# A fused attention, routing and channel-mix kernel: every tile's buffer from a table, routing's compare on GpSimd, and a new hand-written order

## The chip, the cores and the metric

The kernel runs on one core of a Trainium2 chip. The metric is the device time of one execution in microseconds, as the median of several runs. The engines are named TensorE (PE in the profile), VectorE (DVE), ScalarE (ACT), GpSimd (POOL) and SyncE (SP), the last of which only issues transfers here.

## The reference, cut to what matters

Three layers follow each other. The first is attention with hashed buckets, 2 batches, 8 heads, 768 rows, 64 columns a head. The second is a mixture of 4 attention experts with causal masks, of which each row uses the two with the largest gate logits. The third is a channel mix with a hidden width of 1,024.

```python
# layer 1: scores only where the sign bits of q and k under proj agree
q_bits = (einsum('bhsd,dk->bhsk', q, proj) > 0); k_bits = ...
scores = where(q_bucket == k_bucket, q @ k.T / 8, -1e9)
x = softmax(scores) @ v
# layer 2: top 2 of 4 experts by x @ w_gate
for e in range(4):
    a = softmax(causal((x @ wq[e]) @ (x @ wk[e]).T / 8))
    out += gate_weight(e) * (a @ (x @ wv[e]) @ wo[e])
# layer 3: x_prev is x moved down by one row
xk = mu_k * x + (1 - mu_k) * x_prev;  xr = mu_r * x + (1 - mu_r) * x_prev
return sigmoid(xr @ w_r) * (relu(xk @ w_k) ** 2 @ w_v)
```

The weights of layer 3 come as 64-bit floats.

## The kernel before, in words

The rows are worked on in 12 units of 128 (6 per batch). Nearly every matrix is held as the sum of two 16-bit parts, a high one and a low one, so that three 16-bit matmuls give one precise product. A high part is a cast (mostly ScalarE), a low part is a subtraction (VectorE or GpSimd).

The steps of a unit i are these. `prep` and `hash_` (lines 477 to 495) load the query tile, split it (tile `naq`), turn it on TensorE and make hash signs. `score(h)` (line 545) makes one head's scores in PSUM (tile `s`, two slots), and `softmax` (line 518) takes the masked minimum on VectorE (tile `P`), the exponential on ScalarE, the high part (`PHL`), the low part on GpSimd (`PHL<-P,PHL`), and has a transfer turn both (`PT<-PHL`). `pv(h)` (line 562) multiplies with the values (tile `x`). `moe_steps` (line 602) does the same for the experts. Its `proj_v` (line 634) also makes the gate logits in PSUM (tile `vg`) and the routing: VectorE copies the logits out (`lg`), GpSimd subtracts all pairs and adds a constant for ties (`gt`, lines 659 and 660), VectorE compares with zero (line 661) and counts (`rk`, lines 662 and 663), and forms the gate product (`g`, line 666). `mix_steps` (line 768) is layer 3: `shift`, eight `hidden` blocks (matmul tile `h`), four `gate` blocks (`r`) and eight `down` blocks (`v`, into the output tile `e`).

The keys and values of a batch are split once (`key_steps`, line 418): `half` makes the key tiles (`nak`, `nbk`, `y2`), `hash_` their hash signs (`z_k`, which need the split projection `prhl`, lines 285 to 290) and `y1`, and `vals` (line 456) splits the values (`v<-v,v` on VectorE, 128x768, with two inputs in SBUF). The layer-3 weights are put together from their 64-bit halves by `split_d` (line 355): one ScalarE, one GpSimd and four VectorE operations for each of 20 blocks of 128x512, besides a cast.

All operations are first recorded as objects, one list in program order. `arrange` (line 179) reads a table of 2,566 numbers and puts them into the order in which they are issued (`ORDER`, line 865): that order alone sets how the engines' queues interleave, and each engine then works through its own queue in order. Transfers in go through SyncE's queue, except the constants, the projection and the two mixing vectors, which go through ScalarE's queue.

Tiles come from pools. `b2` (2 KB a partition, 18 slots) holds most of a unit's work, `b3` (13 slots) the softmax tiles, `b4` (4 KB, 3 slots) raw weights and the hidden activations `k2`. PSUM has four banks under the tag `d` and two two-bank slots for scores. The layer-3 weights WK2, WV2 and WR have tiles of their own for the whole kernel (40 KB a partition). Before, a tile takes the slot of its tag that the framework gives it at issue.

Of the kernel before, what the change touches and what calls it, by code (L numbers as in the profile page):

```python
# [869 lines left out]
mM|OUKyfUA)o?H5!Jg0_IzSUBi9?_wR>#Kp8`i-C&<5(_J{Uox=q6@>KcNAPp;A~ABhhGzOf_&lG{J+=8#+QGXo|OREak_)VJ`dyw{aYer+Lr<>tQpDLIto5  # L870
7Q{jrmF{3$D2xyA5In^Ba2OupS6l!K;TyKaXw(kg;Su<b1>ISAjGbTuY=k~=7w_Rw_<`r3Ikv)<7?WD#1e!z>={^2Iu_!jhp~+Mq7g1qX)V0I*xR^G<W_XTA
X$$m)#n>6*(s4Ke9q<Eo#9j#W5x2r8JP+~c1r~9|+%|ZLeeoDXr~7yn;uDk51-J;ku@8Fcf}POO6zYndF$p2{$Io~Yp5QAy1;^+gSVG6?HNL^2pwth$VGj(n
l-5yVBKm?)(dc)4i_fqpPNnXclrBL+8iK{$-&Dd4z~PvH#$ZWzg08_bx(p-mIxMH5xSpobSR97qa5|l&2y_Qx&|bO$|G`Zdh~serCZj8`k2cV3ib!{%kSpa9
(N-FXqi`brfg9-*y?3K=65fOT^e>!-IaJyur@3?sw$W|aL@6jGy@4n2tNX=G##A&22jgEf1=G+poQgB(03D<<?hM?A)HILM(+4-7GSPILfirOyK7bYU5Vq4w
%1X6eI!a4FQ$~6OvvCg2#m6uVX3`;AKu;kvWufepgFd-`=ubLK3&~-BHy?j@=V%@-z*Y3oWuP7O*)7CH_!hpp=B}(eLeJniynrS65>`_=w-Ud(7H&0`cY7!&
t-`ZZl=9LV+DW@;7FBTBi18J)bh+q@D?m%}H<ypTJK*J5jF#bfdJXN}7J3Ko;fGsGn@P}P3HlR1zy(@^A3<?|+fA)pLCQ}RU2!T&t=(T(h$^|l^a%#Kb^JG%
qTCelGkk#*_%Bs)$fxNHT_nesC=a!9rRg#m4su_ij;lZ&Tt({Wn6FR+SJhRbYAym2H+1W{2wkOXbc3!_cPD&@%1~MQg}%XHw}Gp>lz5B2Lt8h*MZ`|-KU#~O
T@P2+)pMz^9F?cr)X4n+z%H(_yGfoa(_MN_!yMuZdPOg(iCck$_vk)Vq4!jks?krpk*iZpszJ3VHCA@@T|2jl(_mWM%v*S*+sggiPxzW@xL@fFHFXau64s{3
PPwN`hriKw{zTjO1HGm67#U+=GuPFv#~A!KZp293%YCNaF7QYCLN(nZ>f^prRvzkxyC@hHqhU;p%rQAS)}dIO0FB?#H>&08QzP2JyLbb}=1sVhck^LRh?_AA
$HH|Ofge*n%EommJ0IaD)R;!O9DI}?&@paGTW}k0#~pZ$<MaQc;=a=l+KJs<U-yKz;!}!^&nOY*<XlW{7skOj>|9*D&hfAT9p|{*R?h2$aD(F`J8=nkH}1tf  # L880
# [73 lines left out]
```

## Time and profile before

| what | us |
|---|---|
| median of 3 runs | 506.62 (505.15 to 506.81) |
| the profiled execution, its own time | 508.27 |
| its span, first to last instruction | 506.5 |
| busy in the span: TensorE, VectorE, ScalarE, GpSimd | 440.5, 371.2, 340.8, 317.8 |
| mean granted TensorE clock, as a share of full speed | 0.952 |

In the rows further down, an instruction is named by what it writes and reads (`P<-s`), by names in the program with buffer numbers left out. Line 188 is the one place that issues everything, so all rows have that line and are told apart by their tiles. A time in brackets after `idle before` is how long the engine had nothing to do ahead of it, and the name behind the arrow is what ended it.

### The profile page before, as it was taken

The page shows a single profiled execution, that of the slowest core. Times are in us where ns is not written, and L with a number is a line of the kernel's source. Part 1 is how long each engine was busy: PE and PEld are TensorE (multiplying, and loading weights), DVE is VectorE, ACT ScalarE, POOL GpSimd, SP SyncE. Part 2 cuts the span into 40 slices and gives each one's busy share as a digit, 9 for nine tenths or more (in the row PEclk, how much of TensorE's full clock was granted, in tenths as well). Part 3 has the DMA queues.
Part 4 walks back from the last instruction along what each step waited for, and adds up shares of the span by engine and source line. Part 5 has one row for each costly group of instructions (what it writes and reads, how often), then busy time and mean ns, then how long its engine had stood idle before and what let it go on. Part 6 is the DMA issues. An engine that isn't in the chain of part 4 may idle for free.

```text
span 506.5 us, 15492 instructions
## 1 busy us (share of the span) xinstructions
PE 440.5 (87%) x6288; PEld 334.7 (66%) x6288; DVE 371.2 (73%) x1010; ACT 340.8 (67%) x646; POOL 317.8 (63%) x309
## 2 busy tenths in 40 slices
PE   3663588786879999999989999899899999999996
PEld 2641367574666767767765887587687867886753
DVE  4899788999988867999788579576867554554412
ACT  4259478668887987667868886866786856662411
POOL 2659977775795785857758956745876752452200
PEclk9996578897989999999999999999999999999999
DMA  8699979899989998964989687977983890645011
GB/s 274 165 249 204 174 173 166 217 187 215 167 198 193 180 162 189 182 120 91 156 178 183 128 136 137 150 143 112 160 146 72 135 156 6 106 65 147 1 64 41
DMA packets 224856, 75.06 MB, mean 148 GB/s; under 512 B 216208, under 2 KB 220432, under 8 KB 224784
## 3 DMA queue, kind: packets, MB, share of 16 engines
q1 hardware_dynamic: 223280, 73.95, 76.4%
q8 instruction: 49, 0.80, 0.7%
q10 hardware_dynamic: 1504, 0.11, 0.2%
q14 instruction: 23, 0.19, 0.1%
HBM read 22.14 MB, written 3.15 MB: 50 GB/s over the span
## 4 chain that ended last, share of the span: by engine, by line
PE 46%; DMA 6%; DVE 6%; ACT 4%; issue 3%; POOL 2%; SPq 1%; DVEq 0%; POOLq 0%; ACTq 0%
PE h L188 10%; PE v L188 9%; PE r L188 5%; PE s L188 5%; PE x L188 4%; DMA PT<-PHL 4%; PE qk L188 2%; PE se L188 2%; PE y L188 2%; PE o L188 2%; ACT P L188 2%; PE vg L188 2%; POOL PHL L188 1%; PE tr_y L188 1%; DVE P L188 1%
## 5 line engine op out<-in xcount | busy, mean ns | idle before, releaser
L188 POOL TENSOR_TENSOR PHL<-P,PHL 128x768 f16<-128x768 f32 x96 | 159.0, 1664 | 33.8 <-ACT PHL L188 28.2
L188 DVE TENSOR_SCALAR_CACHE_REDUCE P<-s 128x768 f32<-128x768 f32 x96 | 90.9, 950 | 16.2 <-DMA PT<-PHL 4.8
L188 ACT ACTIVATE P<-P,mx 128x768 f32<-128x768 f32 x96 | 89.1, 929 | 15.8 <-DVE mx L188 15.4
L188 PE MATMUL s<-y,x 128*128 128x384 f16 x384 | 83.2, 348 | 10.9 <-DVE P L188 8.5
L188 PE MATMUL h<-mk,WK 128*128 128x128 f16 x1152 | 75.5, 221 | 3.4 <-DVE WV L188 2.4
L188 PE MATMUL x<-v,PT 128*128 128x64 f16 x1728 | 68.0, 199 | 11.5 <-DMA PT<-PHL 7.3
L188 PEld LDWEIGHTS <-PT 128*128 128x128 f16 x1728 | 63.1, 102 | 20.1 <-DMA PT<-PHL 9.3
L188 PEld LDWEIGHTS <-WK 128*128 128x128 f16 x1152 | 69.2, 99 | 8.5 <-issue 4.1
L188 PE MATMUL v<-WV,k 128*128 128x512 f16 x288 | 71.1, 379 | 0.4 <-DVE WV L188 0.4
L188 PEld LDWEIGHTS <-x 128*128 128x128 f16 x576 | 42.6, 102 | 41.1 <-issue 17.4
L188 ACT ACTIVATE PHL<-P 128x768 f16<-128x768 f32 x72 | 60.1, 837 | 11.9 <-DMA PT<-PHL 3.2
L188 POOL TENSOR_TENSOR PHL_m<-P_m,PHL_m 128x512 f16<-128x512 f32 (+2 forms) x24 | 33.8, 1413 | 27.4 <-ACT PHL_m L188 26.7
L188 PEld LDWEIGHTS <-k 128*128 128x128 f16 x288 | 26.4, 98 | 24.7 <-issue 0.6
L188 PE MATMUL r<-WR,mr 128*128 128x512 f16 x144 | 37.6, 385 | 0.0
L188 PE MATMUL qk<-xT,WQK 128*128 128x128 f16 x576 | 37.2, 219 | 0.3 <-DVE xT L188 0.3
L188 PEld LDWEIGHTS <-WQK 128*128 128x128 f16 x576 | 33.9, 98 | 3.5 <-issue 0.7
L188 POOL TENSOR_SCALAR PHL<-P 128x768 f16<-128x768 f32 x24 | 20.3, 846 | 15.0 <-ACT P L188 7.1
L188 DVE SCALAR_TENSOR_TENSOR h<-h,t 128x512 f32<-128x512 f32 x24 | 16.6, 693 | 13.2 <-ACT t L188 13.1
L188 DVE TENSOR_SCALAR_CACHE_REDUCE P_m<-se 128x512 f32<-128x512 f32 (+2 forms) x24 | 19.4, 818 | 8.8 <-PE se L188 5.0
L188 DVE COPY x<-tr_x 128x512 f16<-128x512 f16 x48 | 19.4, 417 | 6.9 <-PE tr_x L188 6.8
L188 ACT ACTIVATE t<-h 128x512 f32<-128x512 f32 x24 | 14.1, 588 | 14.2 <-PE h L188 13.8
L188 ACT ACTIVATE P_m<-P_m,bias_m 128x512 f32<-128x512 f32 (+2 forms) x24 | 19.7, 821 | 5.7 <-DVE P_m L188 5.5
(133 smaller groups left out, 854.6 us busy)
## 6 DMA issues: line engine op xcount, KB each, us to landing
raw_k<-in_moe_w_k_dram SPq DMA_DIRECT2D x8, 512.0 KB, 4.7
raw_v<-in_moe_w_v_dram SPq DMA_DIRECT2D x8, 512.0 KB, 4.3
q<-in_q_dram SPq DMA_DIRECT2D x12, 256.0 KB, 5.0
k<-in_k_dram SPq DMA_DIRECT2D x8, 384.0 KB, 4.9
v<-in_v_dram SPq DMA_DIRECT2D x8, 384.0 KB, 4.3
...
PT<-PHL SPq DMA_TRANSPOSE x96, 4.2
```

The costliest lines, as they stand in the source:

```text
L188: getattr(getattr(self.nc, engine), method)(*[real(a) for a in args], **{k: real(a) for k, a in kw.items()})
```

## The change

It has six parts.

- `arrange` takes a second table, HOMES, with one number for each tile that has a tag. The tile's tag becomes the tag and that number, with one buffer, so that each tile's slot is set beforehand and not by rotation.
- The weights WK2, WR and WV2 are no longer tiles of their own but 20 blocks of 2 KB in `b2`, which has 40 slots instead of 18. The matmuls read them block by block.
- The hidden activations `k2` are two tiles in `b2` (high and low) instead of one in `b4`, which has 2 slots instead of 3.
- Routing's comparison with zero runs on GpSimd, as a compare and a multiplication by one.
- The ranks are written to a part of the PSUM bank of the value projection (`pw[:, 416:420]`) instead of to SBUF. The gate product reads them there.
- ORDER is a new table for the same operations. It was made by a planner that counts the locks of the port that VectorE and GpSimd share.

```diff
-    def arrange(self, table):
-        places = np.frombuffer(zlib.decompress(base64.b85decode("".join(table.split()))), np.uint16)
-        self.order = [self.ops[i] for i in places]
+    def arrange(self, table, homes):
+        def unpack(text, dt):
+            return np.frombuffer(zlib.decompress(base64.b85decode("".join(text.split()))), dt)
+        self.order = [self.ops[i] for i in unpack(table, np.uint16)]
+        tiles = {}
+        for o in self.ops:
+            for t in o.uses:
+                tiles.setdefault(t, len(tiles))
+        for t, h in zip(tiles, unpack(homes, np.uint8)):
+            if t.slot:
+                t.kw.update(tag=f"{t.slot[1]}_{h}", bufs=1)
...
-    NB2, NB3, NB4, NX2 = 18, 13, 3, 4
+    NB2, NB3, NB4, NX2 = 40, 13, 2, 4
...
-    WK2 = cp.tile([P, NC, 2, DFF], F16, name="WK2")
-    WV2 = cp.tile([P, NF, 2, DM], F16, name="WV2")
-    WR = cp.tile([P, NC, 2, DM], F16, name="WR")
+    WK2, WV2, WR = {}, {}, {}
+
+    def block(d, key, nm):
+        def part(hl):
+            if key not in d:
+                d[key] = sp.tile([P, 2, WN], F16, tag="b2", bufs=NB2, name=nm)
+            return d[key][:, hl, :]
+        return part
...
-                    w_k[c * P:(c + 1) * P, m:m + WN], lambda hl: WK2[:, c, hl, m:m + WN], SWK, f"k2{c}_{m}"))
+                    w_k[c * P:(c + 1) * P, m:m + WN], block(WK2, (c, m), f"WK2_{c}_{m}"), SWK, f"k2{c}_{m}"))
...
-            nc.vector.tensor_scalar(gt, gt, 0.0, None, op0=OP.is_lt)
-            rank = sp.tile([P, E], F32, tag="rk", name=f"rk_{i}")
+            nc.gpsimd.tensor_scalar(gt, gt, 0.0, 1.0, op0=OP.is_lt, op1=OP.mult)
+            rank = pw[:, 416:416 + E]
             nc.vector.tensor_reduce(rank, gt, op=OP.add, axis=mybir.AxisListType.X)
...
-                st["k2"] = sp.tile([P, 2, NF, P], F16, tag="b4", bufs=NB4, name=f"k2_{i}")
+                st["k2"] = [sp.tile([P, NF, P], F16, tag="b2", bufs=NB2, name=f"k2{a}_{i}") for a in "hl"]
...
-                wh, wl = WK2[:, c, 0, cs], WK2[:, c, 1, cs]
+                w = WK2[c, f * P // WN * WN]
+                wh, wl = w[:, 0, cs], w[:, 1, cs]
...
-            nc.tensor.matmul(pv_, k2[:, 0, f, :], WV2[:, f, 0, :], start=(f == 0), stop=False)
+            nc.tensor.matmul(pv_, k2[0][:, f, :], WV2[f][:, 0, :], start=(f == 0), stop=False)
...
-    nc.arrange(ORDER)
+    nc.arrange(ORDER, HOMES)
```

The two tables themselves are compressed text. Unpacked, the first is again a permutation of 2,566 operations, and the second holds 1,283 slot numbers.

## Rows read from the trace of the kernel before

**Rows 1.** The page, part 1: busy us, share of the span and instructions of each engine.

```profile
PE 440.5 (87%) x6288; PEld 334.7 (66%) x6288; DVE 371.2 (73%) x1010; ACT 340.8 (67%) x646; POOL 317.8 (63%) x309
```

**Rows 2.** Windows: stretch, its length, busy us of each engine, clock, DMA share, GB/s.

```profile
0.00:25.00 25.00, 12.34 (x172) 11.24 (x173) 15.99 (x33) 8.83 (x12) 11.14 (x19) 1.00 0.75 219
25.00:170.00 145.00, 107.18 (x1458) 79.99 (x1455) 132.79 (x349) 109.03 (x214) 110.04 (x107) 0.85 0.96 195
170.00:350.00 180.00, 169.82 (x2676) 132.86 (x2674) 141.51 (x402) 137.07 (x261) 127.58 (x118) 0.99 0.87 152
350.00:506.50 156.50, 151.13 (x1993) 110.58 (x1991) 80.89 (x228) 85.84 (x160) 69.04 (x66) 1.00 0.49 89
```

**Rows 3.** Timelines of ACT, DVE and PE, 0 to 16 us: start us, us, instruction.

```profile
6.32 0.53 ACTq L188 DMA_DIRECT2D pr<-in_proj_dram  x1
...
14.06 0.66 DVE L188 CAST prhl<-pr 128x6 f16<-128x6 f32 x1 [2.69 <-DMA pr<-in_proj_dram]
...
15.29 1.44 PE L188 MATMUL z_k<-prhl,y 128*128 128x6 f16 x48 [3.91 <-DVE prhl L188]
```

**Rows 4.** Instructions by tile, whole span: ns least/median/most, first and last start us.

```profile
L188 DVE TENSOR_SCALAR gt<-gt x12: 165/172/1481, 88.2 to 453.6; 128x16 f32<-128x16 f32 x12
...
L188 DVE SCALAR_TENSOR_TENSOR g<-rk,ge x12: 151/154/1210, 100.2 to 460.6; 128x4 f32<-128x4 f32 x12
...
L188 POOL TENSOR_TENSOR gt<-gt,ties x12: 214/220/803, 85.8 to 450.6; 128x16 f32<-128x16 f32 x12
...
L188 DVE SCALAR_TENSOR_TENSOR v<-v,v x8: 959/1620/2387, 40.0 to 258.7; 128x768 f16<-128x768 f32 x8
...
L188 DVE SCALAR_TENSOR_TENSOR naq<-q,naq x12: 681/729/2021, 4.8 to 344.0; 128x512 f16<-128x512 f32 x12
```

**Rows 5.** Timelines of POOL and DVE, 87.9 to 89.6 us.

```profile
87.92 1.64 POOL L188 TENSOR_TENSOR PHL<-P,PHL 128x768 f16<-128x768 f32 x1 [1.01 <-DMA PT<-PHL]
...
88.24 1.35 DVE L188 TENSOR_SCALAR gt<-gt 128x16 f32<-128x16 f32 x1
```

**Rows 6.** Groups on DVE, 0 to 170 us: count | busy us, mean ns | idle before.

```profile
L188 DVE SCALAR_TENSOR_TENSOR v<-v,v 128x768 f16<-128x768 f32 x4 | 7.0, 1763 | 0.0
L188 DVE SCALAR_TENSOR_TENSOR naq<-q,naq 128x512 f16<-128x512 f32 x6 | 4.9, 825 | 4.8 <-ACT naq L188 4.8
...
L188 DVE TENSOR_SCALAR gt<-gt 128x16 f32<-128x16 f32 x3 | 3.3, 1085 | 0.0
```

**Rows 7.** Groups on DVE, 170 to 506.5 us, the same columns.

```profile
L188 DVE SCALAR_TENSOR_TENSOR naq<-q,naq 128x512 f16<-128x512 f32 x6 | 6.9, 1158 | 0.0
L188 DVE SCALAR_TENSOR_TENSOR v<-v,v 128x768 f16<-128x768 f32 x4 | 6.4, 1602 | 1.1 <-ACT v L188 1.0
...
L188 DVE TENSOR_SCALAR gt<-gt 128x16 f32<-128x16 f32 x9 | 3.9, 436 | 1.6 <-POOL gt L188 1.6
L188 DVE SCALAR_TENSOR_TENSOR g<-rk,ge 128x4 f32<-128x4 f32 x9 | 3.4, 375 | 1.8 <-ACT ge L188 1.8
```

**Rows 8.** Timelines: unit 0's routing on DVE and POOL, and one TensorE wait.

```profile
77.77 0.15 DVE L188 TENSOR_SCALAR_CACHE_REDUCE lg<-vg 128x4 f32<-128x4 f32 x1
...
85.82 0.23 POOL L188 TENSOR_TENSOR gt<-gt,ties 128x16 f32<-128x16 f32 x1
...
100.18 0.15 DVE L188 SCALAR_TENSOR_TENSOR g<-rk,ge 128x4 f32<-128x4 f32 x1
...
216.37 0.49 PE L188 MATMUL tr_y<-consts,nbk 128*128 128x128 f16 x6 [1.91 <-DVE rk L188]
```

**Rows 9.** Timelines of DVE and POOL, 203.8 to 205.3 us.

```profile
203.81 1.36 DVE L188 SCALAR_TENSOR_TENSOR nak<-k,nak 128x768 f16<-128x768 f32 x1
...
204.44 0.80 POOL L188 TENSOR_TENSOR gt<-gt,ties 128x16 f32<-128x16 f32 x1
```

**Rows 10.** Waits: engine and tile, what ended the wait, us in total, times, longest.

```profile
PE x L188 <- DMA PT<-PHL: 7.3, 9, 1.9
```

More of the change, by code (lines that the diff above doesn't have):

```diff
@@ L807, in hidden @@
             nc.scalar.activation(t, ph, AF.Relu, scale=sc)
-            hi, lo = k2[:, 0, f0:f0 + 4, :], k2[:, 1, f0:f0 + 4, :]
+            hi, lo = k2[0][:, f0:f0 + 4, :], k2[1][:, f0:f0 + 4, :]
             nc.scalar.activation(hi, t, AF.Square)
@@ L818, in gate @@
             pr = st["pr"]
-            nc.tensor.matmul(pr, x[:, 0, c, :], WR[:, c, 0, :], start=(c == 0), stop=False)
-            nc.tensor.matmul(pr, x[:, 0, c, :], WR[:, c, 1, :], start=False, stop=False)
-            nc.tensor.matmul(pr, x[:, 1, c, :], WR[:, c, 0, :], start=False, stop=(c == NC - 1))
+            nc.tensor.matmul(pr, x[:, 0, c, :], WR[c][:, 0, :], start=(c == 0), stop=False)
+            nc.tensor.matmul(pr, x[:, 0, c, :], WR[c][:, 1, :], start=False, stop=False)
+            nc.tensor.matmul(pr, x[:, 1, c, :], WR[c][:, 0, :], start=False, stop=(c == NC - 1))
             if c == NC - 1:
@@ L831, in down @@
             pv_ = st["pv"]
-            nc.tensor.matmul(pv_, k2[:, 0, f, :], WV2[:, f, 0, :], start=(f == 0), stop=False)
-            nc.tensor.matmul(pv_, k2[:, 0, f, :], WV2[:, f, 1, :], start=False, stop=False)
-            nc.tensor.matmul(pv_, k2[:, 1, f, :], WV2[:, f, 0, :], start=False, stop=(f == NF - 1))
+            nc.tensor.matmul(pv_, k2[0][:, f, :], WV2[f][:, 0, :], start=(f == 0), stop=False)
+            nc.tensor.matmul(pv_, k2[0][:, f, :], WV2[f][:, 1, :], start=False, stop=False)
+            nc.tensor.matmul(pv_, k2[1][:, f, :], WV2[f][:, 0, :], start=False, stop=(f == NF - 1))
             if f == NF - 1:
@@ L870 @@
[L870 to L879, printed above, removed]
@@ L910 @@
-kG->(_SL@GNBd--?Uj|bU+lG&u{ZX`zS|Fj2pEAPxCk7fwNIkwbbJ^}WlbXd4-$GPmj
+c-jq@V;30K7DVqozHu5m4I0~4n>4m<+idIxjoHR&W81cE+xB~ZV7|=kwPrg9uCYUx-u>$GxeV?%_lG;>)lG2cbeJ3EqPZ^a7uVP2cNtxAm(`VY<W75Y1zagt
++Ldu<d~k(bW>?hx?!3$7BDk1tqATPkIdQ{XK^M_Aat&M*m(3M%#T>f}{+y5MF8cF6i<|7qx{7X!%kFZz9B!&B=PI}nF1m~1O1P13n(OCAyZ&x~8w!J5XV=wr
+bAP&AE{_}N&id|diA&>_x;9+PHFdS!V7JUQaV=ddSJ$ngW-hnO>&m-G?k88xRd<zKWf$4Sa<ScXSHfTNzxy~Yu8ZfYxG}DzPvEZj_%4wf>#DlME}<LeQn(~8
+onP)!y30PjU*T%FWUjEU>E7cO*Uq(f`LL94?V7t5uC#CC+PX4+rCa5;y7K<Izv@Ro24BG^cS&7+U(pxwH~i0To7?Uh_@aJ?%jolCT35+e_QiZwU)}d`J>5K4
@@ new lines @@
+*3b8ud}g1;cW_mF9XH?o>QlM#uBu<)e)HLU4WHfbbgNxW|Cd|na`<|#mLCQUeNLat_i}q&ao^mhb9sCuXyg~UYkslo=xY0aU1LAPHSxLqaLDWHyVPzZ-1IGc
+WVq$?`6%$!?{a(HH-FpjcHjLdhzd=89ly`j_0b?Y`~=PX10NI0`O#1S^ZS{ufWPB^`2XB~_b0UWvEYDv=nMK;u8^PYV#7h#$`g!%=f0Z%+qLnJ{6B6ijDx%0
+K^*Aq&bT#>;f0^$=DP9F(ocYT{+++)J;a4RZZ#cp4P88V?4S4{Zm4VP54*oWpq+2;*SdA?y+7-UU?H3b9sE=O!573%?wq^t0pi1am<a3LOW)J?@f+L%D2zq%
+qgQz4lfp*#%pY-|{3h3yyZBYG8an#UJ_#Ix#L&sV_67@~yYK3cy3OvqI}B^!f|~>p0pYXn=fC*L(8K=>fA}~4tq*X__4g5=ukYnAx=U^me86tLw?FPi`@#NC
+Kfn+31N~T^08Y3eek~05WBevK0w>*Nw+nW|W*F+n`BUyF9D^(Fs#^>(AQ2>lnK0h}<wy9DevrT8j>9##4wAtv_z#NVuQ=83fzxi9p90C@H~bx^`w4!EPXV)`
@@ new lines @@
+IHrW_Zj>*HTi_Q+4HNw&e**r68?FTIg}d%=*auT#3EXsPAU)i2HE^=8iML%d%m}Gq8f=BM@DHqq{cz8H#QScB&j1fxI@kaQ;1f=VIq=XOgnl^FpM^~D$j$Ou
+U@828v;AY&95X{U*aq7nJLG^fPzwL{bNw9u8UOL6aTzR!bMOV{`6up;d+V}79{7r<;HjGnGhhX*glBGn|Azni7FY($VmWMyJD~`C$HhJ;Ec7dUE?DlD`n-@2
+miZs}+%59|`FGCId-uZC!u(JkH^NJI9*V-RumdU}lBaff658WwxBx^STnFrrKozk*est)U_=~X4x5C<301CoyPz+wV;;_<Rg4eE~w8l1A2<l*NC;@e`F#Hb5
+{bi_xtNj{(6$bo2{F7tf06XG99E9Q<Vr5kS*_mHMWuXdQfwlfRT!U^Hd?#G*Z$U{Y1Erx9Fnw_me0MAdx1l_2^mm{F2vx-t{s!EH9@rVzQc6D<>tPrC#ovcU
+*b_JSRQ>^cb$6i}K8K<B9@^pvd;v;Euiyhbgh%ig8e<du=Bi_A{|TNz8h;O-LR0L8uc0@_r$|&0D#1%g>myTT_zWN64XpAJeP0}gF=&(j?nYu1N<cr{C`?FI
@@ new lines @@
+VFP8MuDFi+U{v}7&U;@Cs=yG8N#K8`>af{w@mXm&zJ+)26}~|tisWlTWFII3ZKU-S#b=|ael*6SXg-E-EeZT4+UmDZ8cIwxAR1+-=spKMgPc?gHq&<6N<VqP
+AF$2GrtLls#q^C}8|@&(y3hm&(^4$I+kc1uSBDWP7agE_&=BfCZD2e|v3+CM=>>QAUH&TliE(^=P)z9CNL*?FQ81BDLea@^kKgOZU{gp&as440i}Cz5N>2NH
+dyYp*sW*?ar1}#b@CSV!x=!)^et*bE!oxlS?xZ6=Hyx%Ubd+w;O)5qaF<@#cOh<h>O6-&Pr2c20%<rOG)C|Vq1pEuf<1v5SXQmVs8B@}2`h}umblgpODLrMN
+i8vYiaYouhdnpy=qjo$6<KZMc;p1W)%un-hIZnl&Fb4ic(ePi4jWKZ=wuH4<gfh`SDnJD(KK_SGa2?LTnK%n)<5K(^r{jEFf&btfEJQ7!J-nr&)Eqi-2j~bL
+xD%|$4Y&YT;vtNM%WyDvhK=|uEyRx8nTt~wZUrT%D|h2}^an4(->D>>*HyS0hj9Yjj6HcVcIT&boYr6|>c#J=HME5u{DCS{6{<?rs0~!76SNgeQ#m?Do3Iam
@@ new lines @@
+q#86A+rc)hNww$`m8CMY1#44Zu1F_oJMO?!RGxNX9ePHUr~>V$Av~0y(`h<G-QX^Dfv&I%pU^-)N4s$k4&r-spFY#i`hs54S$akLa4+`f{dfQe@Oe6jhw&(0
+pzd&o9#9YH2@mNAp23Usi1zVTeodF?G7aZG&==~_SLz3UKrcw9XR$Y&#$)(@wD~xm!ur%7M({`;#iMyYH=wq1fSb?&_(5;zPySBhc`T3P(%}j{rfuAino=`r
+MD3(5HK&1al(+L3KE{n{5bWTce2@=u3%bvP;V@6+NqmG`QhVCNdwCasp})8Tox_f_n_JN$KF$+(F}Ig*G@VcKX+Fgr<OH{-Hq?naQ(FSQ#2w`vC&bHqfj@C4
+`ImdpdG1LU`7{5=OZWlL;F<h|A2RY8Zb!slIWZ=}N1Ozg@*KXy-}pP9$L=(Xlj3at8P78FW4^+jr3*dbr~Hhs@-@EB-DomT;V#luUU66IMZM`YC&T2J0;BL$
+p2lxDI^X3J_%|=(7#x$I^FRE9U+{ds$FX=WzvZa>6Q9I)Jec0|a*oFHcm>DiIDA1@a!Ops!oO$={RLCudfvdw#(`65YFxz;I1;bslp2{MayslG-K3|a#ngI(
@@ new lines @@
+H*#`a!you2Z{p3omTz%9POE9OyQI@Tbel=y^Gi;TeQ5zF;Dp?dl5kS~nHTaFPOoWj0A;`woRZTrN(Svu1L+USq#3oBWWhm{S%=V2>MeaF9sj~0A2};#!vVq~
+GJ?iXCj65IN*48!h!b;8b&?%tOEON*={W-z;#8cGQ*&HS!-HfPsgwyBF*6R9tU5%7$}s6G{p4@S%qBUov1a02`j3pIoS2m-OA`$eL7M7l%7w$}56Pz4wV7t)
++?t(p@En;UQ)Qau(YZ2D`b!R-FUuv0M3hL9g`>)J8E-SBx#ratnos|-+;{^Q$|8v-i{&QX!aR5z?_gwEAu%Mj<m8odNw4Tw*&qv~wvLnWGE0WbOlhhAN_6>8
+mdGl(s+V<y{3Ii#jxLqIWP+@gm=Z_EQCyiQlO&$Rmjsef63KeGfR{0`T+?4<lx&tH^0UN}G?Ge2%NkiLf67I@h?npRrk13VR({pWdKJ@2GTA7<>2<BE_4FFv
+(Caux(#v?di}&#X-osp6S|4I=uCK`@g`|`Wl80~WBU~pp^(j8XO>#@`XmPEgW%MyV!K&Io^I}8IuLU?i7tm!=P|IpoDWusXFX!WeT$s1WCoQbc@daj-O!5-9
@@ new lines @@
+$}8L^pEbJ_;}Tj;i)c~(U5n{<`IXH|@eV1<ukj6LmYtGCa!6c@XC<|qR@V~zMcZq9dyD0@hE~vBvRiUWF4-d`Ik)`Idu6{IkbN?ezUnufV58`}CNO6QC65F<
+A`$GE9G4T4U-C*VZL5tmpA_MmT2V{sNne^H+9C0FSQ1(RIVwN&j8xLH0W6W7mGg2zBH3>o*@|-%D<mc4r2Iu_#igkHE~liJ6qb_GL5s*anM7A)0$r8sa!p$6
+U2UTiX)?9ab~@1}+a&9#Q*0{Tkc)CjPRkpaLN}!h-;&Fc*lx>odZL|ls!g|PHiPEST$)L<sPq3%$p2?-U34}*kcaYAr_nuqB=>cez1A5P&EDuUeXcL`rOvdw
+@;Ci#f7?Hl+-BQbeW&mBgWi+-(nGuJ9f@u~Sq%Hf9_T!JsE@R_#<cm=M<2@q`lyffjP0?7)K$A_Pd#hBbdL4ais6a$*8zIY_S$eAp_M{X+hXVKsf^Nn_Dn9=
+T$^X*LlTQ)uOybe(%4om4Aen7Sf5LU@T>IG`L@-DXbKyuf9Np1XfI`)F0%<bUKdeRs~oC?#q=-zN6T%YB{Q{@_KQ^w+ibK>)W5WpjMV-1r%uu_y1*{kSY2c*
@@ new lines @@
+YzZx;l{Q%q*g;!sHA2mh%2L}pTW@J>yREX-_Ck(WwXlp{%TYUK%V}sR$1A9Mcq?D!yL^$w)-R;DX_~>NXj+@9W%-c3mv8b;X6i@zAjj>5ZLrK%o@Zz}o30i3
+r0uYsw#!c08rx_Y?T?Vj`iCqwOK0ofn$;@uzm~&tS|zT`Rd|zSv;XXdEwSIN7T4yw{EyDjxjHQDwmMwWvRgUJWw|Yn<+Xga*-BYyo3GccfX&luwm=u^Rl8!v
+>{t8E7Hb(RZof&bP>&mML0hD?!@s&(-{DfL&xP!V3<%||ArB8D!f9*7jk#gCY)$y4H43Y=tQEE*R>F!}Rj$T|ZH?ZtI-xq(;HCPX*5nFS(JI+WU7~eESt&2=
+!!qp<I)+Z+wsj77tVL+bV?xVNPVQP|t7=uOTPP#-LTSlw^~1<8Dpa!yGB6AZU4ql@VQi>wtwKd<9omG(p+^`O#)oItjGJ={er}(nXBZqRNe!!MwXCMJ<W~IB
+DobstBekuT)UgJkZD<#|hS&C4>e?H7YcK4bH3@%(3E`E!w-44dG`5MMS$Jp<tgh6PC-&5;NL8sOK_lor>lJ#3=Aph!4-KTAMbt>zz#?ly8y)(D`}W8lTXktD
@@ new lines @@
+^$o+6&`26f2o(MdjjV|^x4z+{)sW@7LWhK@VRD!hHt4kQ-DZRq_Q~4V%+So*SyTIApY4mS*CsM6%npBt2q9wFq)nxnw6u9)Zde#Nw6?akQU3{>b&GD*IbnX-
+rVB!I@!CQbg*9Pq*c4g{Xmlk--5%EJx*(ywwX#Uzt939|QB~7#7CE@EBWOq*{x8PC!r~BBmxN_uc~}uvhNa=(uqvz$|Aqb*Mf+Jt`@^E?PZ~q_hL{>lH-`Z>
+(Dv&d?PU8jw#LyewpZio`miDF3;V-?a4>8PgKV%3v7bVW5Hmyz@ic0PuTetu5Gx$egSs>93WxNtcDAmzk`m|<J*u%oLX8vRhVItQwuIebPgtj0Lu+m&+rqKX
+!;XhzdR$NFNsSj0X<|(nPU&{tp*!_xND$(OU3w(!)<dDE9S(^?l8`+79Fm4)Aw@_XQiWf_iEuKc38%G}^|n5CDh#z@mNxXYlp$lt5YmTCA#=zQvWDR{!baLC
+I~}rxGvPuwAI@mHP$c9Hc|yK0+WxdLb}pO^`9slAAQTLR!o_eYTn<-5;gCHP3pqm0@N4)j6b~iB@8L?g9<GJk;YPR<?uJ|8Ubq?VhezRI$Q2%h7vXWp9iD_|
@@ new lines @@
+;c0jtK7@DSeRvt(hL7P>_#D23ui;zx9)5)Xi)e&b;dOWuAOc1x`G0jgt7ENH7y?O@Bm56Sktmk
+"""
+HOMES = """
+c-lpj4SO0n41{MS`P&I?2&G4Jl!oQ_|NrpD+|e!%i+8c*SEG>uU0#~gVs<!4Gb9>_?097!dIzg|z1|^f4%Wa-w>7`{H!Z06;NLj#I|jevYX9)f{^H4gYIfpg
+ip#A3J3sIRC;!2Ne<<)TocP91|HK~e82-u?z99=CPhjf9(w$KYqYsXnaN*~F5RZ#h7*>U5EgN24Smm<c*mmJJ#kcTcitl8asF7f9EDBiqaA74PRwCNi^+HLl
+3sqlhoNgfiC2ZafFZwx#z3_^D#1G&XLlA{y4z$@&&Dm2ocnlUR;w0Wp#P&aL<^x_6lZMjK?0CBF4d;S8cJ}4nZ^YYT=*li>#b}tW`1G|^q4mO)JKt@?lb6|<
+LfC;~xkz$%UR_IeC<ou{DjD<;JW}+c9tpEA0%NNMxhg`GpchB-gs|No>UFEq$rrPgn4Y>Lq_!Wu?R+m)&Qkg1%%aeg+PzWOOiCf7_%Lndt)ukHnoYtTjn7N<
@@ L911 @@
+QwmcnsF1xBTmPLwSJ-*y)-EClpLbaT_ZCBsHn}!Z#Z@3llbeRaCwu8=qva%PqfB8dIv!O`Tz2iEi4>Ss#g{_A6MYQWCWl*>>GzBJdQes4Dg!J@&VH4jr3PE4
+L`2NM=tY7q)s<J9iMdHBHvX<p6-v`2b%LJes?500n{Bbf-dAjw*Y;EmbCqz7D{fMrN`vx};tg57C=74@YyfJ4OU<<WX*h}3PnV<n?p6ePhi`t+P4gr!l1kQk
+LZ1>~Ry9HriPCYIZQ~6~&}Tu)kk^*Rong5fx77$S=E-cEepaVn0vGt|*wrvo=SB1?P8BJwglm>7wTtB0<lU#pgj!_Cbv_?u>2tyBgpk^oaX+}|?1UZ1x=9r+
+QRiv_%IX6-c`9k?+a*zzq#^plA3HIvcGiKQw8GOEQjp8~O26n_xE$|3Ro{OB*2Wy^
 """
```

40 lines of the change are left out of this document (3 added, 37 removed).

## The prediction, made before the change was run

> **What bounds the kernel now.** I read the page first [rows 1]: TensorE is busy 440.5 us of 506.5, VectorE 371.2, and as averages these say little. The windows by stretch [rows 2] show that the two change places. Up to 170 us TensorE does 119.5 us of 170 (12.34 + 107.18), with a granted clock of 0.85 from 25 us on, while VectorE is busy 132.8 of 145. From 170 us on TensorE is busy 169.8 of 180 and then 151.1 of 156.5. So the kernel has two stretches: VectorE sets the pace to about 170 us, TensorE after it. The waits at the start say the same: TensorE's first idle stretches end on VectorE [rows 3]. What takes VectorE time off the first stretch should move everything behind it; what takes VectorE time off the second is worth only what TensorE really waited for.
>
> The work itself stays. Both order tables, unpacked, hold the same 2,566 operations; no matmul, no weight and no transfer is added or dropped, and ScalarE switches between Exp and Sigmoid as often. A profiled execution took 508.27 us around its span of 506.5, the median of the runs is 506.62 (505.15 to 506.81): I take the gains off the span and carry the same gain to the median.
>
> **Part 1, the start.** Before, the two small loads of the projection stand on ScalarE's queue behind the first key and query casts, the first at 6.32 us; VectorE's cast of it starts at 14.06 after 2.69 us of idleness, and TensorE's first hash matmul waits 3.91 us [rows 3]. The new order issues both ahead of every cast. What is late next is the second key half of group 0, whose load goes from 7th to 11th on SP's queue (the gate weights, a query tile nine units early, an output weight and a raw weight now go ahead of it). Ends: nothing, if that half now holds the hash, and 3.9 us. I take the 2.7 us of VectorE idleness, since VectorE is the bound there. **-2.7.**
>
> **Part 2, routing's compare to GpSimd, ranks to PSUM.** VectorE's compare of 16 elements takes 172 ns at the median and 1,481 at the most, and its gate product 154 and 1,210 [rows 4]. The long ones are waits inside the instruction: unit 0's ran for 1.35 us, to the end of a GpSimd subtraction that had begun before it [rows 5]. Up to 170 us the three compares cost 3.3 us, later the nine cost 3.9 and the nine gate products 3.4 [rows 6, 7]. The compare leaves VectorE whole: -3.3 early (its free duration included). The reduction that reads the compare's result stays; with ranks in PSUM the gate product has one SBUF input left, and I let it fall to its 154 ns. Late, that is 3.9 + 9 x (0.375 - 0.154) = 5.9 us of VectorE, but TensorE waited for this chain only where the rank ended its 1.91 us wait at 216 us [rows 8], so I count 2.0. On GpSimd a compare of this size has no row; its own second step on that tile takes 220 ns at the median [rows 4], so I take 0.21 us with one input fewer, 12 times that is 2.5 us; the ends are nothing and the 0.80 us of its longest step each time, 9.6 us. GpSimd had 35 us idle in the first stretch [rows 2]: nothing on the path by itself. **-5.3.**
>
> A row shows that such a wait works in both directions: the second GpSimd routing step of unit 4 took 0.80 us where unit 0's took 0.23, while VectorE ran a two-input subtraction beside it [rows 9]. The Trainium skill, page SBUF — State Buffer, section "Who interferes with whom", says that VectorE and GpSimd share a port pair as an exclusive lock, held for the whole instruction by whoever starts first. By that rule the moved compare may still lose, now on GpSimd's side, and the part would give less than counted; the trace agrees that the loser can be GpSimd. With 0.58 us (0.80 - 0.22) lost in every unit and a third of that on the path, the sum would be -9.5 by that rule.
>
> **Part 3, order around the other long waits.** The value split (v) takes 1,763 ns early and 1,602 late where 959 is its least, the query split 825 and 1,158 where 681 is the least [rows 4, 6, 7]. That is 4 x 0.80 + 6 x 0.14 = 4.1 us early and 4 x 0.64 + 6 x 0.48 = 5.4 late. These operations keep their engine, so only the order can spare them. Ends: nothing, and all 9.5. The tables alone can't show which will still meet a GpSimd operation, so I take half of the early part, and 0.6 late, some tenth, since VectorE isn't the bound there. **-2.7.**
>
> **Part 4, the rest of the order and the buffers.** I added up, for both tables, the VectorE work that must be over before given matmuls (each operation at its traced duration, the long waits trimmed). Ahead of unit 0's first down matmul it falls from 143.5 to 141.4 us, ahead of the 60th us of TensorE work from 105 to 99, and after that the two tables run within 6 us of each other, in both directions. I take the 2.1. Giving each tile a slot by table has no row: its gain is at most the transfer waits that TensorE shows, 7.3 us on attention's probabilities [rows 10], its loss as much, if a slot that frees late can't be passed over. I count 0. The raw-weight slots fall from 3 to 2 and the hidden activations move to the common pool; the pool keeps 20 slots beside the weights where it had 18 and one of three larger ones held those activations, so that is even, and before the weights arrive there are more. **-2.1.**
>
> **Part 5, the new wait.** VectorE's rank now waits for GpSimd's third routing step instead of its second, and is placed sooner: in unit 0 the gate product came 22.4 us after the logits [rows 8]. Between logits and gate the old table has 15.3 us of VectorE work per unit (mean of 12), the new one 4.1. Behind the waiting rank stand the masked minima of the scores, which free TensorE's score banks. GpSimd's second step ended 8.3 us after the logits began in unit 0 [rows 8], mostly behind subtractions. The new table also moves the steps together (GpSimd work from the first to the end of the third: 0.4 us in five units, 4.2 at most, 1.5 in the mean, where first to second alone held 2.9), so I count only 1.0 for the first three units; the ends are nothing and the price of (b) below. The bank of the value projection is held until the gate; with the gate placed early that is some 1.2 us of VectorE work longer per unit, and I count nothing, covered by the other three banks. **+1.0.**
>
> Sum: -2.7 - 5.3 - 2.7 - 2.1 + 1.0 = -11.8. Span 494.7; the median 506.6 - 11.8 = 494.8, rounded to **495.0 us**.
>
> **Rivals.** (a) *Transfers set the first stretch.* The DMA engines' share is 0.96 from 25 to 170 us [rows 2]; if that is a limit and not just queued packets, VectorE's savings become waits for loads and transposes; the start and the late 2.6 leave 501.3, the late part alone 504.0, and nothing 506.6: taken as 504. Against it: TensorE waited only 7.3 us in all for transposes of attention [rows 10].
> (b) *GpSimd's lag blocks VectorE: slower.* If the routing steps lag as in unit 0 (8.3 us) while the cover is 4.1 us, each unit stops VectorE for some 4.2 us at the rank, in order, with score minima behind it. Twelve times 4.2 is 50 us; from 350 us on VectorE has 75 of 156 us free [rows 2], so I put a third of it, 17 us, on the path, instead of 1.0: 495 + 16 = 511. It decides where the third routing step ends more than 4 us after the logits in most units. For it: GpSimd's steps queue behind its subtractions. Against it: the steps stand closer together in the new table, and unit 11, with 0.2 us of cover, has them back to back.
> (c) *The early stretch gives more.* All early waits go (4.1 + 3.3), the start gives 3.9, the order the 6 us it shows at the 60th us of TensorE work, and with fewer holes the clock of 0.85 rises; with the late 2.6 that is 20 us and more: 478 to 489.
> (d) *It doesn't do what it says:* the long waits only move to other pairs of operations. Then parts 1 and 4 remain, 501.8; this lies with (a).
>
> **Numbers.** A measurement tells this kernel from no change at about 0.3% (1.5 us). The forecast (489 to 502) gets 0.50, (c) 0.12, (a) and (d) together 0.20, (b) 0.18. Of (a) and (d) half lies below 505.1, so faster 0.72, within 0.3% 0.10, slower 0.18. The range leaves out the upper half of (b) and the lower half of (c): 484 to 509; the forecast's own range is 489 to 502.
>
> **What would show it.** Right: VectorE's projection cast before 10 us; no compare and no gate product over 0.3 us on VectorE; the value split's mean near 1.3 us; the first down matmul some 9 us earlier, and from there to the end the same time within 3 us. Wrong: long idle times of VectorE ended by GpSimd's routing tile (b); VectorE less busy than 125 of the 145 us from 25 to 170 with its idle times ended by transfers (a); a gain after 170 us larger than the one before it, which would say that the second stretch was not bound as I read it.

## The result and the profile after

The changed kernel takes **485.24 us** (median of 4 runs, 482.02 to 488.85) where the kernel before, on the same chip, takes 505.88 (504.55 to 506.81): a ratio of 0.9596, 95% interval 0.952 to 0.9671. That is 20.6 us less, where 11.8 were forecast. The profiled execution took 486.35 us around a span of 484.2. One per cent of 505.88 is 5.06 us, and ratios are turned into us by it in all that follows.

Part 1 of the page after, to be held against [rows 1]:

```profile
PE 435.3 (90%) x6288; PEld 331.9 (69%) x6288; DVE 355.0 (73%) x998; ACT 338.6 (70%) x646; POOL 322.6 (67%) x321
```

VectorE lost 12 instructions, the compares, and 16.2 us of busy time, GpSimd won the 12 and 4.8 us. TensorE's own 5.2 us come with its mean granted clock, 0.967 after and 0.952 before, on the same 6,288 matmuls.

The windows after, with the columns of [rows 2]:

```profile
0.00:25.00 25.00, 15.24 (x222) 12.64 (x222) 17.86 (x40) 10.21 (x14) 13.77 (x24) 1.00 1.02 282
25.00:170.00 145.00, 113.05 (x1588) 84.85 (x1588) 134.28 (x365) 119.04 (x233) 118.71 (x115) 0.89 1.05 202
170.00:350.00 180.00, 176.73 (x2801) 140.12 (x2798) 139.49 (x424) 139.89 (x272) 136.16 (x128) 1.00 0.81 149
350.00:484.20 134.20, 130.30 (x1684) 94.28 (x1681) 63.34 (x172) 69.48 (x129) 53.95 (x56) 1.00 0.45 89
```

The number in brackets behind TensorE's time counts its matmuls. By 170 us the kernel before had done 172 + 1,458 = 1,630, the changed one 222 + 1,588 = 1,810: 180 ahead. By 350 us the two stood at 4,306 and 4,611: 305 ahead. Matmuls differ in length, but the count shows that the lead still grows in the stretch that the prediction took to be TensorE's own.

Instructions by tile, with the columns of [rows 4]. The kernel before's down matmuls first; below, of the changed kernel, the down matmuls by the high part, the value split, and routing's steps:

```profile
L188 PE MATMUL v<-WV,k x288: 376/379/381, 163.3 to 502.2; 128*128 128x512 f16 x144
```
```profile
L196 PE MATMUL v<-WV,k2h x192: 376/379/380, 154.6 to 479.7; 128*128 128x512 f16 x192
L196 DVE SCALAR_TENSOR_TENSOR v<-v,v x8: 949/1228/2405, 37.7 to 240.7; 128x768 f16<-128x768 f32 x8
...
L196 POOL TENSOR_TENSOR gt<-lg x12: 207/216/864, 76.4 to 417.9; 128x16 f32<-128x16 f32 x12
L196 POOL TENSOR_TENSOR gt<-gt,ties x12: 211/222/226, 76.7 to 418.2; 128x16 f32<-128x16 f32 x12
L196 POOL TENSOR_SCALAR gt<-gt x12: 272/273/978, 83.4 to 418.5; 128x16 f32<-128x16 f32 x12
...
L196 DVE SCALAR_TENSOR_TENSOR g<-vg,ge x12: 150/162/165, 84.5 to 419.5; 128x4 f32<-128x4 f32 x12
```

Unit 0's first down matmul starts at 154.6 us instead of 163.3. Those 8.7 us are what the prediction named ("some 9 us earlier"). From there to the end of the span the kernel before takes 506.5 - 163.3 = 343.2 us and the changed one 484.2 - 154.6 = 329.6. These 13.6 us were to be under 3. So the early part came as forecast, and the larger part of the gain came where none was counted. The prediction had named this as a sign of being wrong ("a gain after 170 us larger than the one before it"). Where the larger part came from, the runs had to tell.

### The profile page after: what moved, and what is told of

The parts are those of the page before. It is cut to its first block, busy times and chain, and to the rows that moved or that the text cites. A ratio compares the mean times of both kernels' runs of the same rounds, so it can differ in the third digit from the quotient of the medians.

```text
span 484.2 us, 15510 instructions
## 1 busy us (share of the span) xinstructions
PE 435.3 (90%) x6288; PEld 331.9 (69%) x6288; DVE 355.0 (73%) x998; ACT 338.6 (70%) x646; POOL 322.6 (67%) x321
## 4 chain that ended last, share of the span: by engine, by line
PE 57%; DVE 12%; DMA 12%; POOL 8%; issue 6%; ACT 4%; SPq 0%; POOLq 0%; DVEq 0%; ACTq 0%
PE h L196 11%; PE v L196 11%; PE s L196 7%; PE x L196 6%; PE r L196 5%; POOL PHL L196 5%; DMA PT<-PHL 5%; PE qk L196 4%; PE se L196 3%; PE o L196 3%; DVE P L196 2%; PE y L196 2%; PE vg L196 2%; DMA raw_k<-in_moe_w_k_dram 2%; DVE wd_v L196 2%
## 5 line engine op out<-in xcount | busy, mean ns | idle before, releaser
L196 POOL TENSOR_TENSOR PHL<-P,PHL 128x768 f16<-128x768 f32 x96 | 160.9, 1684 | 27.1 <-ACT PHL L196 22.0
L196 PE MATMUL x<-v,PT 128*128 128x64 f16 x1728 | 65.8, 197 | 11.5 <-DVE WK L196 6.4
L196 PE MATMUL h<-mk,WK 128*128 128x128 f16 x1152 | 73.2, 219 | 0.4 <-DVE x L196 0.4
L196 PEld LDWEIGHTS <-WK 128*128 128x128 f16 x1152 | 67.1, 98 | 4.8 <-DVE x L196 1.0
L196 PE MATMUL v<-WV,k2h 128*128 128x512 f16 x192 | 57.1, 379 | 0.0
L196 POOL TENSOR_TENSOR mk<-m32k,mk 128x512 f16<-128x512 f32 x12 | 13.9, 1159 | 41.5 <-ACT mk L196 41.4
L196 PE MATMUL qk<-xT,WQK 128*128 128x128 f16 x576 | 36.9, 219 | 1.7 <-DVE kT L196 1.1
L196 PE MATMUL v<-WV,k2l 128*128 128x512 f16 x96 | 36.4, 379 | 0.0
L196 PE MATMUL r<-WR,mr 128*128 128x512 f16 x144 | 35.8, 379 | 0.0
L196 ACT ACT_TABLE_LOAD x16 | 20.5, 1283 | 12.0 <-issue 7.6
L196 PEld LDWEIGHTS <-k2h 128*128 128x128 f16 x192 | 16.7, 98 | 11.7
```

Of the source, the lines that this page charges most:

```text
L196: getattr(getattr(self.nc, engine), method)(*[real(a) for a in args], **{k: real(a) for k, a in kw.items()})
```

## Experiments

Each was timed beside the kernel before, on the same chip; ratios are to that one, with the 95% interval in brackets.

### Compare and order, one at a time

The first has the kernel before with one line changed:

```diff
-            nc.vector.tensor_scalar(gt, gt, 0.0, None, op0=OP.is_lt)
+            nc.gpsimd.tensor_scalar(gt, gt, 0.0, 1.0, op0=OP.is_lt, op1=OP.mult)
```

> The kernel before with one edit: routing's compare on GpSimd (the ranks stay in SBUF, order and buffers are the old ones). Theory A (the prediction's part 2): the compare leaves VectorE with its long waits, -3.3 us early and some 1 to 2 us late: 501 to 503 us. Rival B (the order carries nearly the whole gain, the compare alone only moves a wait to GpSimd's queue): within 1.5 us of the kernel before. Rival C (the rank waits for a third GpSimd step behind the old order's subtractions): slower than before, 507 us or more.

Ratio 0.998 (0.9961 to 0.9999), some 1.0 us less: theory A counted too much, B fits.

The second has the kernel before with only the text of ORDER replaced, the third the new ORDER and the line above.

> The kernel before with the new order table alone (compare on VectorE, ranks in SBUF, old buffers, slots by the framework). Theory A (parts 1, 3 and 4 as predicted, -7.5 us): 497 to 500 us. Rival B (the order carries nearly the whole gain of 20.6 us): 485 to 489 us. Rival C (the gain beyond the prediction comes from the buffers by table): 497 us or more, and the next kernel too.

> The kernel before with the new order table and the compare on GpSimd (ranks in SBUF, old buffers, slots by the framework). If order and compare together carry the gain: 485 to 488 us. Rival C (the buffers by table and the weights in the common pool carry the 8.8 us that the prediction missed): 493 to 497 us.

The order alone is **slower** than the kernel before, ratio 1.0206 (1.0167 to 1.0246); only theory C's open end ("497 us or more") holds it. With the compare moved it is 1.0077 (1.0042 to 1.0111), above both ranges that its own expectation set. So the compare is worth 1.0206 - 1.0077 = 1.3%, 6.5 us, in the new order, and 1.0 in the old one. What the compare meets there stands in the rows of the routing tile in the order-only kernel, and below them of the gate product in the kernel with the compare moved:

```profile
L188 DVE TENSOR_SCALAR gt<-gt x12: 165/175/1598, 81.8 to 450.1; 128x16 f32<-128x16 f32 x12
...
its engine sat idle before it (us, times) until:
  POOL gt L188: 11.7, 6
```
```profile
L188 DVE SCALAR_TENSOR_TENSOR g<-rk,ge x12: 162/695/1482, 82.4 to 439.9; 128x4 f32<-128x4 f32 x12
```

In the new order the compare follows its producer so closely that VectorE stands still 11.7 us for GpSimd's second step, and still meets GpSimd's subtractions (1,598 ns at the most). In the kernel before, it had waited 1.6 us for that step [rows 7]. The gate product is long as well: a mean of 636 ns in the order-only kernel and of 756 (695 at the median) with the compare moved, where the kernel before has 319. The changed kernel, which reads the ranks from PSUM, has a mean of 159 and no instance over 165, and the kernel without the table of slots below has 158 and 163. The Trainium skill, page SBUF — State Buffer, section "Who interferes with whom", says that a VectorE operation with two SBUF inputs contends with a GpSimd operation that reads SBUF. The two gate products agree with it: 756 ns in the mean with two inputs there, 159 with one. No run moved the ranks alone.

### Everything but the table of slots

```diff
-            if t.slot:
+            if False:
                 t.kw.update(tag=f"{t.slot[1]}_{h}", bufs=1)
```

> The changed kernel without the table of slots (the framework gives each tile its slot; 40 slots in the common pool, everything else as changed). Prediction's part 4 (slots by table count 0): 484 to 487 us. Rival C (the table of slots carries the missed 8.8 us): 493 to 495 us.

Ratio 0.9976 (0.9947 to 1.0005): without the table the other five edits come to nothing that can be told from no change, above rival C's 493 to 495 us and far above the prediction's 484 to 487. The windows of this kernel:

```profile
0.00:25.00 25.00, 14.80 (x218) 12.47 (x219) 16.99 (x37) 10.31 (x14) 14.08 (x24) 1.00 1.00 267
25.00:170.00 145.00, 110.21 (x1544) 83.54 (x1541) 134.29 (x354) 114.84 (x224) 113.64 (x112) 0.88 1.01 198
170.00:350.00 180.00, 167.41 (x2626) 129.88 (x2624) 135.27 (x409) 134.29 (x262) 129.76 (x123) 1.00 0.82 143
```

At 170 us it has done 1,762 matmuls, 132 more than the kernel before, so most of the early lead (180 with the table) is there without it; at 350 us it has 4,388, and the lead is down to 82. The new order wins early and gives much of it back between 170 and 350 us. The chain of waits of this kernel shows one place of the kind that costs time, from 357 us on (start us, us, what):

```profile
357.83 0.74 ACT PHL L196
358.57 0.07 issue
358.64 0.24 POOL PHL L196
358.88 3.81 DMA PT_m_p<-PHL_m_p
...
362.77 0.85 ACT PHL L196
363.63 0.07 issue
363.70 2.44 POOL PHL L196 x2
...
366.22 1.66 POOL PHL L196
367.88 0.02 issue
367.90 0.04 DVE P L196
```

ScalarE's cast at 362.77 makes the high part (PHL) of one head's softmax and is released by the transfer that turns an expert's tile, PT_m_p. It needs no data of that transfer. So what it needs must be the slot: its tile was put where that transfer's source lay. Then GpSimd's low parts come late, and VectorE's next score minimum waits for GpSimd, whose data it does not need either. Such waits can be read off the table of waits: no writer of P, PHL, nak or nbk (ScalarE, VectorE, GpSimd) reads what a transposing transfer makes, so where such a transfer ended its idle time, it waited for a slot. All these rows of the table of waits, without the table of slots and with it (engine, tile, releaser: us in total, times, longest):

```profile
ACT PHL L196 <- DMA PT<-PHL: 8.4, 8, 1.9
...
ACT nak L196 <- DMA PT<-PHL: 4.7, 1, 4.7
ACT PHL L196 <- DMA PT_m_p<-PHL_m_p: 2.8, 1, 2.8
...
POOL PHL L196 <- DMA PT_m_p<-PHL_m_p: 2.2, 1, 2.2
DVE P L196 <- DMA PT<-PHL: 2.1, 2, 1.2
DVE P L196 <- DMA PT_m_p<-PHL_m_p: 2.1, 2, 1.6
...
POOL PHL_m L196 <- DMA PT_m<-PHL_m: 1.2, 1, 1.2
POOL PHL L196 <- DMA PT<-PHL: 1.2, 1, 1.2
...
ACT nak L196 <- DMA PT_m<-PHL_m: 1.2, 1, 1.2
ACT PHL_m L196 <- DMA PT<-PHL: 0.5, 1, 0.5
DVE P_m_p L196 <- DMA PT<-PHL: 0.3, 1, 0.3
```
```profile
ACT PHL L196 <- DMA PT<-PHL: 2.3, 4, 1.3
ACT PHL_m L196 <- DMA PT<-PHL: 1.8, 1, 1.8
DVE P L196 <- DMA PT<-PHL: 0.6, 1, 0.6
```

They add up to 26.7 us in 20 waits without the table and 4.7 in 6 with it. Of the 26.7, 17.6 lie between 170 and 350 us, where the lead is lost.

### Which slots

The table kept for some tags only, the other tags' slots given by the framework. The edit of the first (the others have `== "d"` and `!= "b3"`):

```diff
-            if t.slot:
+            if t.slot and t.slot[1] == "b3":
```

> The changed kernel with the table of slots kept for the 13 slots of b3 alone (softmax tiles P, PHL, PT, the key and value splits); every other tag's slots are the framework's. Theory D (a b3 slot given by the framework is one that a transposing transfer still reads, and ScalarE's and VectorE's queues stop behind it): most of the 20 us comes back, 485 to 491 us. Rival E (the four PSUM banks d carry it): 500 to 505 us. Rival F (all tags add a little): 494 to 499 us.

> The changed kernel with the table of slots kept for the four PSUM banks d alone. Theory D: 500 to 506 us, as without the table. Rival E: 485 to 491 us. Rival F: 497 to 503 us.

> The changed kernel with the table of slots for all tags but b3. Theory D: 500 to 505 us. Rival E: 485 to 490 us. Rival F: 490 to 497 us.

| slots by table | ratio (95% interval) | waits of ScalarE, VectorE and GpSimd ended by a transposing transfer, us |
|---|---|---|
| none | 0.9976 (0.9947 to 1.0005) | 26.7 |
| PSUM banks d only | 0.9971 (0.994 to 1.0001) | 36.6 |
| all but b3 | 0.9987 (0.9958 to 1.0016) | 36.9 |
| b3 only | 0.9657 (0.9623 to 0.9692) | 8.4 |
| all (the changed kernel) | 0.9596 (0.952 to 0.9671) | 4.7 |

Theory D holds from both sides: b3 alone brings 0.9976 - 0.9657 = 3.2%, 16.1 us, and all the other tags without it bring nothing. What the other tags add on top of b3, 0.6%, lies within the two intervals. The waits tell where to look, but their sum is no price: 26.7 and 36.9 us of them cost the same time.

### The compare back, in the changed kernel

The changed kernel with the compare on VectorE again (the first diff, reversed).

> The changed kernel with routing's compare back on VectorE (ranks stay in PSUM, table and order as changed). Prediction's part 2 (5.3 us, most of it the compare): 489 to 492 us. Theory D with the order planned around the compare's new engine, as the two runs with the new order and without the table differed by 6.7 us: 490 to 494 us. Rival (the compare alone is worth 1.3 us, as with the old order): 486 to 488 us.

Ratio 0.979 (0.9765 to 0.9816): 0.979 - 0.9596 = 1.9%, **9.8 us** lost (5.8 to 13.8 with the two intervals combined), more than each theory had at the point, while the interval reaches into both of the first two ranges. The slot waits stay away (4.8 us); what comes back is on VectorE:

```profile
L196 DVE TENSOR_SCALAR gt<-gt x12: 164/175/1602, 80.4 to 425.5; 128x16 f32<-128x16 f32 x12
...
its engine sat idle before it (us, times) until:
  POOL gt L196: 8.8, 7
```

### A table for the old order

The kernel before, its 428 b3 tiles put into slots by a table made from its own trace; then with the compare on GpSimd as well. The text of HOMES_B3 is left out here.

```diff
         self.order = [self.ops[i] for i in places]
+        tiles = [t for t in dict.fromkeys(t for o in self.ops for t in o.uses) if t.slot and t.slot[1] == "b3"]
+        for t, n in zip(tiles, np.frombuffer(zlib.decompress(base64.b85decode("".join(HOMES_B3.split()))), np.uint8)):
+            t.kw.update(tag=f"b3_{n}", bufs=1)
```

> The kernel before (old order, compare on VectorE, old buffers) with one edit: the slots of its softmax tiles b3 come from a table of our own, made from the traced durations of the kernel before: each tile goes to the slot that was freed last before the tile is needed. Theory D (the framework's choice of b3 slots costs time in either order: ScalarE, VectorE and GpSimd wait 20 us in all there for slots that transfers still read): 491 to 498 us. Rival G (the table only mends what the new order breaks, as the new order without it was no faster than before): within 1.5 us of the kernel before.

> As the run before, with routing's compare on GpSimd as well (ranks in SBUF). Theory D: 1 us less than the run before, 490 to 497 us, so that 5 to 11 us are left for the new order. Rival H (the order is worth nothing by itself; compare and b3 slots are all): 484 to 488 us. Rival G: 504 to 506 us.

Ratios 1.0001 (0.9972 to 1.0029) and 0.999 (0.9955 to 1.0025): nothing, as rival G said. But the runs do not settle it, since our table did not do what it was for. The same rows of the table of waits add up to 17.4 us in the kernel before (the expectation said 20), to 21.4 with our table and to 28.8 with the compare moved as well. The two largest of the kernel before and, below, of the first of the two runs:

```profile
DVE P L188 <- DMA PT<-PHL: 4.8, 2, 2.7
...
ACT PHL L188 <- DMA PT<-PHL: 3.2, 3, 2.0
```
```profile
DVE P L191 <- DMA PT<-PHL: 6.7, 5, 2.8
ACT PHL L191 <- DMA PT<-PHL: 6.2, 4, 2.9
```

The table only took down what TensorE's matmuls wait for transposes, from 8.8 us to 3.3, and that brought no time. Whether a table that spares the old order these waits would gain anything stays open.

### The projection's loads late again

```diff
         self.order = [self.ops[i] for i in unpack(table, np.uint16)]
+        for d in (2, 3):
+            o = self.ops[d]
+            self.order.remove(o)
+            self.order.insert(self.order.index(self.ops[60]) + 1, o)
```

> The changed kernel with one part of the order undone: the two loads of the projection stand on ScalarE's queue behind the first query and key casts again. Prediction's part 1 (2.7 us): 487 to 489.5 us. Rival (a lead of some us at 25 us is swallowed by VectorE's later waits): within 1.5 us of the changed kernel, 484 to 487 us.

Ratio 0.9694 (0.965 to 0.9737), 1.0% or 5.0 us above the changed kernel (0.5 to 9.4 with the two intervals combined; they overlap). The timelines of the changed kernel and, below, of this one:

```profile
1.19 0.54 ACTq L196 DMA_DIRECT2D pr<-in_proj_dram  x1
...
7.81 0.17 DVE L196 CAST prhl<-pr 128x6 f16<-128x6 f32 x1
...
14.18 1.42 PE L196 MATMUL z_k<-prhl,y 128*128 128x6 f16 x48 [0.25 <-DVE y L196]
```
```profile
7.44 1.74 ACTq L200 DMA_DIRECT2D pr<-in_proj_dram  x2
14.70 0.67 DVE L200 CAST prhl<-pr 128x6 f16<-128x6 f32 x1 [6.73 <-DMA pr<-in_proj_dram]
```

VectorE stands idle for 6.73 us here, against 2.69 in the kernel before [rows 3], because the new order reaches the cast sooner. TensorE's first hash matmul starts at 21.58 us here, at 14.18 in the changed kernel and at 15.29 in the kernel before [rows 3]. So the run undoes more than part 1 removed: it shows the sign, and part 1's own size was not measured.

### Both tables made anew

From the changed kernel's order, operations were moved one to four at a time wherever a pass over traced durations said that the end comes sooner, with slots planned in the same pass. Only the two tables' texts differ.

> The changed kernel with both tables made anew together: from its order, single operations are moved by some dozen places at a time and each tile is given the slot that was freed last before it is needed, from the traced durations of the changed kernel; a VectorE split that would run into a GpSimd operation counts against a move. Theory (order and slots act only together, and before 170 us the changed kernel still has 41 us of TensorE idleness): 472 to 482 us. Rival I (what is left there is VectorE's work and the loads, which no order spares): within 1.5 us of the changed kernel, 484 to 487 us. Rival J (traced durations do not carry over to another order, and new collisions take the place of the old): 488 us or more.

Ratio **1.0726** (1.0683 to 1.0768), 57 us slower than the changed kernel, which is rival J's range. Rival J's reason is not shown. Our pass gave each transfer the time that it had taken in the changed kernel, and for the transposes that carried over: attention's take 4.1 us from issue to landing at the median here and 4.0 there, the experts' 3.5 and 4.3 here and 3.7 and 3.7 there. Much is lost early, as the windows of this kernel show:

```profile
0.00:25.00 25.00, 7.37 (x110) 6.51 (x110) 9.53 (x21) 6.77 (x9) 7.15 (x14) 1.00 0.87 226
25.00:170.00 145.00, 99.89 (x1388) 75.09 (x1389) 123.06 (x335) 102.49 (x202) 105.00 (x112) 0.89 0.91 182
```

By 170 us 1,498 matmuls are done where the changed kernel has done 1,810, and TensorE has stood idle for 62.7 us instead of 41.7. Over the whole span the waits for transposes are longer too:

```profile
PE x L196 <- DMA PT<-PHL: 12.8, 7, 5.1
...
DVE P L196 <- DMA PT<-PHL: 12.3, 6, 4.1
```

The changed kernel has 4.4 and 0.6 us in these two rows. The slot waits behind transfers are back at 29.8 us, but the kernel without the table has 26.7 of them and is 38 us faster than this one, so they are not the whole of it. Which of the moved operations did it was not tried, and the cause stays open.

## Why the prediction was right and where it failed

The direction was right, and 485.24 us lies in the recorded range of 484 to 509, 1.2 us above its lower end. It lies outside of the forecast's own 489 to 502: 495.0 was 9.8 us too high. The runs with the new order make a chain from before to after, each step by its ratio: new order +10.4 us, compare to GpSimd -6.5, ranks to PSUM together with weights and hidden activations in the common pool -5.1, table for b3 -16.1, table for the rest -3.1 (this last one within its noise). Another order of the steps would give other sizes: the compare is 9.8 at the end of the chain.

That the number fell into the range was in part luck. The edits that were counted, at -11.8 us together, come to 1.2 us (0.9947 to 1.0005) without the table of slots. The table, which was counted as nothing, brings the other 19.2. What the prediction had right is the early stretch: 8.7 us by unit 0's first down matmul, where it had said some 9. By its steps:

- **The step that failed is in part 4**: "Giving each tile a slot by table has no row: its gain is at most the transfer waits that TensorE shows, 7.3 us on attention's probabilities ... I count 0." In the new order it is worth 16.1 us for b3 alone. The bound was taken on the wrong engine. A slot is held by the transfer that reads its old tile, and what waits is the next *writer*: ScalarE's cast, VectorE's minimum, GpSimd's low part. TensorE's own waits for transposes do not hold it. Rows of this kind were there in the kernel before (17.4 us of such waits), in the same table as [rows 10]. What they cost in the old order is not shown.
- **The reading of the second stretch** failed with it. "TensorE is busy 169.8 of 180" [rows 2] was taken as TensorE's pace, and only the late pieces of parts 2 and 3, 2.6 us, were counted there. After, it is 176.73 of 180 and 130.30 of the last 134.2: TensorE's idle time from 170 us on went from 10.2 + 5.4 to 3.3 + 3.9, 8.4 us less. A share of 94% is not a bound when 15.6 us remain.
- **The other parts of part 4, and part 3**, stood for what the order brings. By itself the order costs 10.4 us (second run). Its trace has more of both waits than the kernel before, 29.4 us to 17.4 for slots behind transfers and 11.7 to 1.6 of the compare for its producer; that these two make up the whole loss is argued, not shown. That the long waits of the splits would get shorter came true in the changed kernel: the value split's mean went from 1,683 ns to 1,397 ("near 1.3 us"), and with query and key splits VectorE is spared 6.0 us (8 x 0.286 + 12 x 0.182 + 8 x 0.195). In the kernel without the table the same sum is 1.3 us (8 x 0.056 - 12 x 0.074 + 8 x 0.217), so the new order without its slots hardly spares these collisions. What of the 6.0 reached the end was not separated.
- **Part 2** had the right mechanism and too small a size. No compare is left on VectorE and no gate product is over 165 ns, as named. It was priced at 5.3 us with the old order's waits; in the new order the compare alone is 6.5 us without the table and 9.8 with it (the intervals of the two overlap), and the gate product's mean fell from 756 ns in the third run to 159 (12 x 0.597 = 7.2 us of VectorE), most likely through the ranks in PSUM. With the old order the compare is worth 1.0: an edit's price depends on the order it stands in. The other outcome that was weighed, 0.58 us lost on GpSimd's side in every unit, did not come: of the 36 routing steps on GpSimd two were long, 864 and 978 ns, and the second step took 226 at the most.
- **Part 1**: right in kind; VectorE's cast starts at 7.81 us ("before 10"). TensorE's first hash matmul came forward by only 1.1 us, to 14.18, and waits for VectorE's copy of a key tile now (`y`, 0.25 us); by 25 us TensorE has done 15.24 us of work instead of 12.34. The 2.7 that was counted was not measured by itself.
- **Part 5** and rival (b): the rank does wait for GpSimd, 5.9 us in 4 waits of VectorE, not 50. The third step ends more than 4 us after the logits' copy in 4 units of 12, not in most (11.7 us at the most, in unit 0; 1.0 at the least). And the wait takes an old one's place rather than adding to it: with the compare back on VectorE, the compare waits 8.8 us in 7 waits for GpSimd's second step, in the same order and with the same table.
- **Rivals (a), (c), (d)**: transfers do not set the first stretch, their share rose to 1.05 while 180 more matmuls were done, and VectorE is busy 134.28 of the 145 us, above the 125 that was to show (a). (c) has the time (478 to 489), but not the way: the early stretch gave 8.7 us, what the forecast had. (d) is out: the long waits did not only move, as VectorE's busy time fell by 16.2 us in all.
